# A place of its own for each of 4935 operations in a fused top-k attention and SoLU kernel

## Chip, cores and metric

The kernel runs on one core of one Trainium2 chip. The metric is the device time of one execution in microseconds. The core's engines, each with a queue of its own, are TensorE (PE, with its weight loads shown as PEld), ScalarE (ACT), VectorE (DVE), GpSimd (POOL) and SyncE (SP), which issues the DMAs.

## What is computed

Attention over 8 batches and 8 heads with 576 positions of 64 features, where each query keeps only its 32 largest scores; then a block of two matrix products (512 to 1024 to 512) for 4608 tokens, with SoLU and a layer norm between. Shortened:

```python
scores = (1 / 8) * q @ k.T                       # per batch and head, 576 x 576
kth = np.partition(scores, -32, axis=-1)[..., -32:-31]
attn = softmax(np.where(scores >= kth, scores, -1e9))
x = (attn @ v)                                   # heads side by side: 4608 x 512
h = x @ w_in                                     # 512 x 1024
solu = h * softmax(h)
ln = (solu - mean(solu)) / np.sqrt(var(solu) + 1e-6) * g_ln
out = ln @ w_out                                 # 1024 x 512
```

The weights arrive as 64-bit floats and are turned into 32-bit floats on the chip.

## The kernel before

**Steps.** `steps_of` cuts the attention into 32 steps, four per batch. A step takes four blocks of 128 queries (two heads each) and one block of tails, nine score tiles of 128x576 in all, numbered j. `work_of` lists the operations of all steps, with the engine of each, its length, what it must come after, and the buffers it uses. Within a step they are, by line of the kernel:

- `prep_q`, `prep_k`, `prep_t`: PE transposes the inputs into one of two PSUM buffers `tp` (tails into `o`); ACT copies them out and squares them.
- `estimate` (L1938, ten pairs of small matmuls), `length` (L1945, DVE), `root` (L1952, POOL), `begin` (L1957, DVE): a first guess of each row's threshold.
- `scores` (L1984, PE into two PSUM buffers `big`), `evac` (L1993, ACT copies to `X`), `exps` (L2115, ACT).
- `count0` (L2001 on DVE, L2009 on ACT): how many scores lie above the guess; `second`, `moved`, `even` (L2027, L2036, L2043, DVE): the guess corrected; `twice` (L2051).
- `count1` (L2058, nine on ACT): signs and count at the new guess; `side` (L2067, DVE, tile `al`, three for three counts each), `nearest` (L2079) and `best` (L2090): the scores next to it; `merged`, `which`, `chosen`, `kth`: the 32nd score.
- `keep` (L2160, DVE): the exponentials above the threshold, with their sum; `inverse`; `turn_r`, `copy_r`, `rd_out`, `rd_in`: the inverse sums go through DRAM to be spread over partitions.
- `transpose_p` and `transpose_last` (L2237, L2268 to L2272, PE into `tp`), `copy_p` and `copy_last` (L2250, L2253, L2276, ACT to `PT`), `attn_v` (L2293), `attn_t` (L2302, PE), `copy_v` (L2316, L2323, DVE to `xTm`, `xTt`).

**Tokens.** For each of 36 blocks of 128 tokens: `mm1` (L2334), `hexp` (L2345), `solu` (L2353), `square` (L2363), `spread` and `ln` (POOL), `transpose_ln` (L2384), `copy_ln` (L2390), `mm2` (L2395), `store` (L2402), `send`. They follow the steps of their batch and overlap the attention of the next.

**Weights.** 16 pieces: `load_w`, `w_bits` and `w_corr` (DVE, L1723 to L1739), `w_sum` (L1746, PE into `tp`), `w_copy` (ACT, L1753). At the end they are loaded again and checked (`w_again`, `w_exp`, `w_check`), and `w_verdict` (L2426) decides whether the general path behind the fast one is run; it isn't with these inputs.

**What sets the order.** `arranged(work, rank)` plays the list through while the kernel is built: each engine takes, among the operations that could start soonest, the one with the lowest rank. `PATIENCE` says how much later than the soonest an operation may start and still be taken, and `TURNING` is added to the rank of a PE operation that uses the array in another way than the last one (mode `f` the whole array, `r` two row halves, `c` two column halves). The result is one list; the kernel makes its instructions in that list's order. For PE, ACT, DVE and POOL it is kept as written, as a fixed order in each engine's queue. The rank of an operation is a base (36000 times its step) and a place from the table `PLACES`. The table has rows of its own for the first 8 pairs of heads, 5 tokens and 4 steps and for the last steps and tokens; all others share one row per kind (the keys one per position among four pairs), so that the steps in the middle repeat one pattern.

Of the kernel before, what the change touches and what calls it, by code (L numbers as in the profile page):

```python
# [470 lines left out]
SINGLE = ()  # L471
# [22 lines left out]
def work_of(B, NP, steps, NF, w_wide):  # L494
# [7 lines left out]
    add = w.add  # L502
# [7 lines left out]
    for b in range(B):  # L510
        for hp in range(NP):
            n = pair(b, hp)
# [12 lines left out]
    for i, (b, chunks) in enumerate(steps):  # L525
# [7 lines left out]
        add(("estimate", i), "PE", 450,  # L533
# [94 lines left out]
    tokens = []  # L628
# [32 lines left out]
    for n in range(NW):  # L661
        if w_wide:
# [5 lines left out]
            add(("w_sum", n), "PE", 1290, [("w_corr", n)], [solu, ("tp", ("w", n))], mode="f")  # L668
# [19 lines left out]
STEP = 36000  # L688


def base_of(steps, tokens):
    firsts = {}
    for i, (b, chunks) in enumerate(steps):
        for c in range(4):
            firsts.setdefault(NPAIR * b + chunks[c][0], i)

    def base(key):
        kind, n = key[0], key[1] if len(key) > 1 else 0
        if kind in KEY_KINDS:
            return firsts[n] * STEP  # L700
        if kind in TOKEN_KINDS:
            b, t = tokens[n][:2]
            if b in SINGLE and t < NPAIR:
                return (NPAIR * b + 1 + t) * STEP
            return (NPAIR * b + 2 + min(t, NPAIR - 1)) * STEP
        if kind in LATE_KINDS:
            return len(steps) * STEP
        if kind in WEIGHT_KINDS:
            return 0
        return n * STEP  # L710

    return base


def class_of(key, tokens):
    kind, n = key[0], key[1] if len(key) > 1 else 0
    if kind in KEY_KINDS:
        return f"K{n}" if n < OWN_KEYS else f"k{n % NPAIR}"
    if kind in TOKEN_KINDS:
        b, t = tokens[n][:2]  # L720
        return f"T{n}" if n < OWN_TOKENS else f"Z{t}" if b == 7 and LAST_OWN else "tt" if t == NPAIR else "t"
    if kind in LATE_KINDS or kind in WEIGHT_KINDS:
        return "w"
    return f"S{n}" if n < OWN_STEPS else f"Z{n}" if n >= 30 and LAST_OWN else "s"


def rank_of(steps, tokens):
    base = base_of(steps, tokens)

    def rank(key):  # L730
        c = class_of(key, tokens)
        n = key[1:] if c == "w" else key[2:]
        return base(key) + PLACES[key[0]][c][n[0] if n else 0]

    return rank


NPAIR = 4
OWN_KEYS = 8
OWN_TOKENS = 5  # L740
OWN_STEPS = 4
LAST_OWN = True
KEY_KINDS = ("load_k", "load_t", "tail_square", "load_v", "prep_t", "prep_tc", "prep_k", "prep_kc", "key_square", "key_stats")
TOKEN_KINDS = ("mm1", "hexp", "solu", "square", "spread", "ln", "transpose_ln", "copy_ln", "mm2", "store", "send")
WEIGHT_KINDS = ("load_g", "turn_g", "copy_g", "load_w", "w_bits", "w_corr", "w_sum", "w_copy", "w_gain")
LATE_KINDS = ("w_again", "w_exp", "w_check", "w_passed", "w_verdict")


def arranged(work, rank):
# [23 lines left out]
    while len(start) < len(ops):  # L773
# [55 lines left out]
    "load_k": {  # L829
        "K0": [-1716811],  # L830
        "K1": [-245828],
        "K2": [227792],
        "K3": [-1429884],
        "K4": [-8176],
        "K5": [-3062009],
        "K6": [-1412841],
        "K7": [-355373],
        "k0": [-1030779],
        "k1": [-1442591],
        "k2": [-382990],  # L840
        "k3": [-303896],
    },
    "load_t": {
        "K0": [-1925714],
        "K1": [102180],
        "K2": [351217],
        "K3": [-2648411],
        "K4": [-204768],
        "K5": [-790824],
        "K6": [-509905],  # L850
        "K7": [-633496],
        "k0": [-1338629],
        "k1": [185959],
        "k2": [439884],
        "k3": [-364413],
    },
    "load_v": {
        "K0": [540359],
        "K1": [-296512],
        "K2": [361785],  # L860
        "K3": [-4133787],
        "K4": [119830],
        "K5": [-3768809],
        "K6": [-444902],
        "K7": [-1875983],
        "k0": [-70963],
        "k1": [-1466686],
        "k2": [422237],
        "k3": [-978377],
    },  # L870
    "prep_t": {
        "K0": [-1084188],
        "K1": [-1474755],
        "K2": [436197],
        "K3": [-2991661],
        "K4": [261520],
        "K5": [-8410692],
        "K6": [-269545],
        "K7": [-1284952],
        "k0": [-91862],  # L880
        "k1": [-4832167],
        "k2": [116192],
        "k3": [-1082843],
    },
    "prep_tc": {
        "K0": [-175869],
        "K1": [-749576],
        "K2": [695963],
        "K3": [-590749],
        "K4": [156084],  # L890
        "K5": [-5714526],
        "K6": [515895],
        "K7": [481801],
        "k0": [-18883],
        "k1": [-2857382],
        "k2": [531774],
        "k3": [412231],
    },
    "prep_k": {
        "K0": [22470],  # L900
        "K1": [517997],
        "K2": [206630],
        "K3": [855959],
        "K4": [311821],
        "K5": [515333],
        "K6": [-897320],
        "K7": [558498],
        "k0": [354441],
        "k1": [550664],
        "k2": [55262],  # L910
        "k3": [749511],
    },
    "prep_kc": {
        "K0": [-705698],
        "K1": [-763489],
        "K2": [532998],
        "K3": [-575397],
        "K4": [-76495],
        "K5": [-4692927],
        "K6": [-1267314],  # L920
        "K7": [631286],
        "k0": [-517929],
        "k1": [-1529512],
        "k2": [-275145],
        "k3": [350554],
    },
    "key_square": {
        "K0": [191609],
        "K1": [429176],
        "K2": [760863],  # L930
        "K3": [113498],
        "K4": [256344],
        "K5": [-1494524],
        "K6": [201870],
        "K7": [101078],
        "k0": [253669],
        "k1": [293599],
        "k2": [343170],
        "k3": [792546],
    },  # L940
    "tail_square": {
        "K0": [76491],
        "K1": [-735608],
        "K2": [1119556],
        "K3": [-1902133],
        "K4": [381088],
        "K5": [-6092744],
        "K6": [874126],
        "K7": [-334823],
        "k0": [441766],  # L950
        "k1": [-3610787],
        "k2": [1220737],
        "k3": [-277945],
    },
    "key_stats": {
        "K0": [-37826],
        "K1": [39185],
        "K2": [713784],
        "K3": [-703728],
        "K4": [352435],  # L960
        "K5": [-1754043],
        "K6": [1022931],
        "K7": [84658],
        "k0": [197438],
        "k1": [-1051412],
        "k2": [786942],
        "k3": [-12787],
    },
    "load_q": {
        "S0": [-156811],  # L970
        "S1": [88026],
        "S2": [-178771],
        "S3": [-241569],
        "s": [-131498],
        "Z30": [217192],
        "Z31": [-163285],
    },
    "prep_q": {
        "S0": [-153430],
        "S1": [74761],  # L980
        "S2": [-544548],
        "S3": [-262135],
        "s": [-36141],
        "Z30": [114],
        "Z31": [-408351],
    },
    "prep_qc": {
        "S0": [-97802],
        "S1": [37948],
        "S2": [51332],  # L990
        "S3": [-101542],
        "s": [-100332],
        "Z30": [-417100],
        "Z31": [29777],
    },
    "query_square": {
        "S0": [1057034],
        "S1": [1050943],
        "S2": [1006679],
        "S3": [814969],  # L1000
        "s": [1193871],
        "Z30": [830474],
        "Z31": [906169],
    },
    "estimate": {
        "S0": [-352846],
        "S1": [61002],
        "S2": [-381815],
        "S3": [37651],
        "s": [-110145],  # L1010
        "Z30": [-174418],
        "Z31": [-370193],
    },
    "length": {
        "S0": [104761],
        "S1": [481856],
        "S2": [313281],
        "S3": [306525],
        "s": [70425],
        "Z30": [-20069],  # L1020
        "Z31": [131569],
    },
    "root": {
        "S0": [-449277],
        "S1": [-186121],
        "S2": [-235754],
        "S3": [-268864],
        "s": [-296482],
        "Z30": [-476424],
        "Z31": [-165276],  # L1030
    },
    "begin": {
        "S0": [-966568],
        "S1": [-845257],
        "S2": [-1066062],
        "S3": [-482811],
        "s": [-533664],
        "Z30": [-1047582],
        "Z31": [-1088684],
    },  # L1040
    "scores": {
        "S0": [-121302, -924421, -715935, -656232, -1101903],
        "S1": [-474433, -984979, -614471, -429193, -118328],
        "S2": [-992219, -774707, -474374, -231896, -220838],
# [1466 lines left out]
```

## Time and profile before

| | us |
|---|---|
| median of 3 runs | 1246.11 (1245.06 to 1247.51) |
| profiled execution | 1244.19 |
| span of its records | 1242.4 |

| engine | busy in the middle, 186 to 1178 us (992 us) | busy in the first 31 us | in the last 33 us |
|---|---|---|---|
| PE | 960.2 | 18.2 | 26.0 |
| DVE | 892.2 | 13.8 | 2.6 |
| ACT | 843.7 | 21.8 | 9.3 |
| POOL | 121.2 | 3.3 | 3.9 |

A profile is one execution. A row of it names a line, an engine, an operation, the written and read tiles, and a count; then its busy time, the mean duration of one, and how long the engine stood idle just before such an instruction, with what ended that idle time. The DMAs moved 64.57 MB, a mean of 52 GB/s, with the DMA engines busy for at most seven tenths of any of the page's 40 slices.

### The profile page before, as it was taken

The page shows a single profiled execution, that of the slowest core. Times are in us where ns is not written, and L with a number is a line of the kernel's source. Part 1 is how long each engine was busy: PE and PEld are TensorE (multiplying, and loading weights), DVE is VectorE, ACT ScalarE, POOL GpSimd, SP SyncE. Part 2 cuts the span into 40 slices and gives each one's busy share as a digit, 9 for nine tenths or more (in the row PEclk, how much of TensorE's full clock was granted, in tenths as well). Part 3 has the DMA queues.
Part 4 walks back from the last instruction along what each step waited for, and adds up shares of the span by engine and source line. Part 5 has one row for each costly group of instructions (what it writes and reads, how often), then busy time and mean ns, then how long its engine had stood idle before and what let it go on. Part 6 is the DMA issues. An engine that isn't in the chain of part 4 may idle for free.

```text
span 1242.4 us, 19028 instructions
## 1 busy us (share of the span) xinstructions
PE 1158.2 (93%) x5868; PEld 656.7 (53%) x5868; DVE 1059.5 (85%) x3113; ACT 1014.7 (82%) x2180; POOL 144.6 (12%) x167
## 2 busy tenths in 40 slices
PE   5586899999999999989999999989999999999997
PEld 3354454555555555555555555555555555554553
DVE  4889999989888988999879888999888888999920
ACT  7799868788887797999877898899877899888642
POOL 1100020201011020210112010110112001120110
PEclk9789999999999999999999999999999999999999
DMA  7321202011120112120120111211120011111510
GB/s 188 90 75 43 88 20 63 11 31 48 47 55 20 38 50 63 33 52 23 35 77 19 39 30 48 64 39 40 30 72 19 31 28 39 56 59 64 171 53 29
DMA packets 111434, 64.57 MB, mean 52 GB/s; under 512 B 90445, under 2 KB 98906, under 8 KB 111322
## 3 DMA queue, kind: packets, MB, share of 16 engines
q1 hardware_dynamic: 111322, 63.25, 18.4%
q8 instruction: 49, 0.80, 0.3%
q14 instruction: 63, 0.52, 0.2%
HBM read 53.65 MB, written 9.57 MB: 51 GB/s over the span
## 4 chain that ended last, share of the span: by engine, by line
PE 59%; ACT 22%; DVE 15%; issue 2%; DMA 0%; POOL 0%; ACTq 0%; DVEq 0%; SPq 0%
PE o_ps L2395 15%; PE h_ps L2334 14%; PE s_ps L1984 9%; PE om L2293 8%; PE tp_p L2237 6%; ACT sg L2058 4%; ACT X L1993 4%; DVE E L2160 3%; DVE w L2090 3%; ACT E L2115 3%; ACT PT L2250 3%; DVE w L2079 3%; DVE junkv L2001 2%; PE om L2302 2%; ACT junka L2009 2%
## 5 line engine op out<-in xcount | busy, mean ns | idle before, releaser
L2395 PE MATMUL o_ps<-w_out,lnT 128*128 128x512 f32 x576 | 257.5, 593 | 0.4 <-DVE xTt L2323 0.2
L2334 PE MATMUL h_ps<-w_in,xTm 128*128 128x512 f32 x512 | 229.3, 593 | 1.6 <-ACT X L1993 1.6
L2090 DVE MAX8 w<-w 128x8 f32<-128x288 f32 x576 | 225.9, 447 | 0.4
L2058 ACT ACTIVATE sg<-X,t 128x576 bf16<-128x576 f32 x256 | 196.9, 775 | 18.3 <-DVE t L2043 18.3
L2079 DVE SCALAR_TENSOR_TENSOR w<-X,al,sg 128x576 f32<-128x576 f32 x256 | 204.8, 824 | 2.1 <-ACT junka L1771 1.1
L1993 ACT ACTIVATE X<-s_ps 128x576 f32<-128x576 f32 x256 | 162.2, 660 | 50.4 <-PE s_ps L1984 48.9
L2160 DVE SCALAR_TENSOR_TENSOR E<-X,kth,E 128x576 f32<-128x576 f32 x256 | 200.5, 814 | 1.8 <-ACT E L2115 0.6
L2001 DVE TENSOR_SCALAR_CACHE_REDUCE junkv<-X,t 128x576 bf16<-128x576 f32 x216 | 174.6, 808 | 16.4 <-ACT X L1993 8.0
L1984 PE MATMUL s_ps<-kT,qT 64*128 64x288 f32 x1024 | 167.3, 435 | 3.7 <-ACT X L1993 3.7
L2237 PE MATMUL tp_p<-ident,E 128*128 128x128 f32 x1024 | 154.3, 280 | 17.7 <-ACT PT L2250 5.7
L2395 PEld LDWEIGHTS o_ps<-w_out,lnT 128*128 128x128 f32 x576 | 105.0, 190 | 111.9 <-issue 109.9
L2250 ACT COPY PT<-tp_p 128x512 f32<-128x512 f32 x256 | 148.2, 596 | 9.7 <-PE tp_p L2237 9.3
L2237 PEld LDWEIGHTS tp_p<-ident,E 128*128 128x128 f32 x1024 | 116.2, 142 | 74.0 <-issue 30.8
L2115 ACT ACTIVATE E<-X 128x1152 f32<-128x1152 f32 x128 | 149.6, 1179 | 0.4 <-PE tp_p L2237 0.2
L2334 PEld LDWEIGHTS h_ps<-w_in,xTm 128*128 128x128 f32 x512 | 93.0, 190 | 99.3 <-issue 96.3
L2293 PE MATMUL om<-PT,vm 128*64 128x256 f32 (+1 forms) x1024 | 139.0, 417 | 6.6 <-DVE t L1957 3.0
L1984 PEld LDWEIGHTS s_ps<-kT,qT 64*128 64x128 f32 x1024 | 94.1, 189 | 59.6 <-issue 26.1
L1952 POOL TENSOR_TENSOR zs<-zs,phalf 128x9 f32<-128x9 f32 x32 | 60.3, 1885 | 459.4 <-DVE zs L1945 459.4
L2293 PEld LDWEIGHTS om<-PT,vm 128*64 128x64 f32 x1024 | 69.6, 138 | 63.4 <-issue 12.7
L2369 POOL TENSOR_SCALAR var<-var 128x1 f32<-128x1 f32 x36 | 11.4, 318 | 608.0 <-ACT e_sb L2363 595.0
L2363 ACT ACTIVATE e_sb<-solu,nmu 128x1024 f32<-128x1024 f32 x36 | 41.3, 1149 | 27.3 <-DVE nmu L2357 23.8
L2067 DVE SCALAR_TENSOR_TENSOR al<-n,tt 128x3 f32<-128x3 f32 x96 | 15.0, 157 | 55.9 <-ACT sg L2058 55.8
(144 smaller groups left out, 1526.2 us busy)
## 6 DMA issues: line engine op xcount, KB each, us to landing
km<-in_k_dram SPq DMA_DIRECT2D x32, 256.0 KB
q_sb<-in_q_dram SPq DMA_DIRECT2D x128, 64.0 KB
vm<-in_v_dram SPq DMA_DIRECT2D x32, 256.0 KB
out_dram<-osb SPq DMA_DIRECT2D x32, 256.0 KB
scales<-rows SPq DMA_DIRECT2D x58, 128.0 KB
w_raw<-in_moe_w_in_dram SPq DMA_DIRECT2D x8, 512.0 KB
w_raw<-in_moe_w_out_dram SPq DMA_DIRECT2D x8, 512.0 KB
w_again<-in_moe_w_in_dram SPq DMA_DIRECT2D x8, 512.0 KB
```

The source lines that it names most:

```text
L1984: nc.tensor.matmul(out=big[h][:, half, 0:SH], lhsT=queries_of(i, t)[hd, :], rhs=kT[hd, k0 : k0 + SH], start=True, stop=True,)
L1993: nc.scalar.activation(out=x_of(i, j).rearrange("p (a s) -> p a s", a=2), in_=d.pop(("s", j))[:, :, 0:SH], func=AF.Copy, scale=scale,)
L2001: nc.vector.tensor_scalar(out=junk, in0=x_of(i, j), scalar1=st[i][t][:, j : j + 1], scalar2=None, op0=ALU.is_ge, op1=ALU.add, accum_out=co ...
L2058: nc.scalar.activation(out=d["sg", j], in_=x_of(i, j), func=AF.Sign, scale=-(1.0 + 2.0**-23), bias=d["t1"][:, j : j + 1], accum_out=column ...
L2079: nc.vector.scalar_tensor_tensor(out=w, in0=x_of(i, j), scalar=d["al"][:, j : j + 1], in1=d.pop(("sg", j)), op0=ALU.subtract, op1=ALU.mult,)
L2090: nc.vector.max(w8[:, j, 8 * half : 8 * half + 8], w[:, half * SH : (half + 1) * SH])
L2115: nc.scalar.activation(out=d["E", t], in_=d["X", t], func=AF.Exp)
L2160: nc.vector.scalar_tensor_tensor(out=e, in0=x_of(i, j), scalar=d["kth"][:, j : j + 1], in1=e, op0=ALU.is_ge, op1=ALU.mult, accum_out=den_a ...
L2237: nc.tensor.transpose(tp[:, c, :], e[:, c * P : (c + 1) * P], ident)
L2293: nc.tensor.matmul(out=o[h * D : (h + 1) * D, cols], lhsT=vm[:, h, c, :], rhs=pt[:, h * NM + c, :], start=(c == 0), stop=False,)
L2334: nc.tensor.matmul(out=h[:, half, :], lhsT=x[:, c, :], rhs=w_in[:, c, half * 512 : (half + 1) * 512], start=(c == 0), stop=(c == NP - 1),)
L2395: nc.tensor.matmul(out=o, lhsT=d["lnT"][:, c, :], rhs=w_out[:, c, :], start=(c == 0), stop=(c == NF - 1),)
```

## The change

`rank_of` with its bases and shared rows is taken out. `PLACES` now holds one number for each operation, found by the operation's own key, and that number alone is its rank. `PATIENCE` and `TURNING` become 0, so that among the operations that could start soonest the lowest place wins. Two lengths in the planner's list are set anew. `arranged`, the makers of the instructions, the buffers and the dependences stay.

```diff
-        add(("estimate", i), "PE", 450,
+        add(("estimate", i), "PE", 300,
...
-            add(("w_sum", n), "PE", 1290, [("w_corr", n)], [solu, ("tp", ("w", n))], mode="f")
+            add(("w_sum", n), "PE", 1560, [("w_corr", n)], [solu, ("tp", ("w", n))], mode="f")
...
-    def rank(key):
-        c = class_of(key, tokens)
-        n = key[1:] if c == "w" else key[2:]
-        return base(key) + PLACES[key[0]][c][n[0] if n else 0]
...
+def place_of(key):
+    places = PLACES[key[0]]
+    for n in key[1:]:
+        places = places[n]
+    return places
...
 PLACES = {
...
-    "side": {
-        "S0": [-1225990, -1004058, -1472440],
-        "S1": [-907195, -897390, -974162],
-        "S2": [-988574, -699495, -808215],
...
+    "side": [
+        [50837, 816, -28229],
+        [-18683, 69915, 58524],
+        [197812, 57921, 126612],
...
-PATIENCE = {"PE": 171, "ACT": 56, "DVE": 0, "POOL": 18243, "SP": 1014}
-TURNING = 352098
+PATIENCE = {"PE": 0, "ACT": 0, "DVE": 0, "POOL": 0, "SP": 0}
+TURNING = 0
...
-        for kind, *args in arranged(work, rank_of(steps, order_of_tokens)):
+        for kind, *args in arranged(work, place_of):
```

The lists that result differ all along, by small moves. The first loads that SP issues, as an example: before km, the tails (q, then k), w_raw, km, q_sb; after it w_raw, the tails, km, q_sb, w_raw. On PE the first operations before are prep_t.0, prep_k.0, scores.0, prep_k.1, prep_q.0, w_sum.0, two of scores.0, prep_t.1, estimate.0; after it prep_t.0, prep_k.0, w_sum.0, prep_q.0, two of scores.0, prep_k.1, scores.0, prep_t.1, w_sum.1, estimate.0.

## The prediction

> **What bounds the kernel now.** Forecast: about 15 us less, 1231 us. The page's busy times, slices and chain come first.
>
> ```profile
> span 1242.4 us, 19028 instructions
> ...
> PE 1158.2 (93%) x5868; PEld 656.7 (53%) x5868; DVE 1059.5 (85%) x3113; ACT 1014.7 (82%) x2180; POOL 144.6 (12%) x167
> ...
> PE   5586899999999999989999999989999999999997
> ...
> DVE  4889999989888988999879888999888888999920
> ...
> PEclk9789999999999999999999999999999999999999
> ...
> PE 59%; ACT 22%; DVE 15%; issue 2%; DMA 0%; POOL 0%; ACTq 0%; DVEq 0%; SPq 0%
> ```
>
> Three engines share the load: PE holds most of the chain but ACT and DVE 37% of it, so it changes engine again and again. Next the table by stages, for the steady part alone:
>
> ```profile
> 186.00:1178.00 992.00, 960.20 (x4907) 546.60 (x4907) 892.15 (x2628) 843.74 (x1807) 121.21 (x119) 1.00 0.17 46
> ```
>
> PE is busy 960.2 of 992 us and idle 31.8. Here a rule speaks **against** the change: an engine 97% busy has nothing to win from order. The Trainium skill (Perfetto Trace Analysis, Identifying the Most-Contended Engine) says that matmul busy time is no measure of PE's headroom, because matmuls are pipelined. The timeline of the tail agrees:
>
> ```profile
> 1190.77 13.90 PE L2334 MATMUL h_ps<-w_in,xTm 128*128 128x512 f32 x32
> ```
>
> 32 of these take 13.90 us, so one starts every (13.90 - 0.59)/31 = 429 ns, though the page gives 593 ns as its duration. By such start intervals (429 ns at 512 columns, 243 at 288, 109 at 128, 25 for an estimate, half for the paired heads) all of PE's work is 1047 us, and 885 us in the steady part. So 107 us of it is not work: 50 us stand at the 270 changes between the array's three uses (whole array, row pairs, column pairs), some 150 ns each in the median, which leaves 56 us of waits. By the busy row order can win at most 32 us there, by the intervals 107; I use the second.
>
> The waits, from the groups by line (busy, mean ns, then idle before and who ended it):
>
> ```profile
> L1993 ACT ACTIVATE X<-s_ps 128x576 f32<-128x576 f32 x256 | 162.2, 660 | 50.4 <-PE s_ps L1984 48.9 <-ACT lnT L2390 0.5 <-ACT Et L2115 0.3
> ...
> L2237 PE MATMUL tp_p<-ident,E 128*128 128x128 f32 x1024 | 154.3, 280 | 17.7 <-ACT PT L2250 5.7 <-ACT PT L2276 5.1 <-ACT PT L2253 1.6
> ...
> L2067 DVE SCALAR_TENSOR_TENSOR al<-n,tt 128x3 f32<-128x3 f32 x96 | 15.0, 157 | 55.9 <-ACT sg L2058 55.8
> ```
>
> and from the list of who waited for whom (total, times, longest):
>
> ```profile
> PEld tp_p L2237 <- ACT PT L2250: 18.3, 35, 1.1
> ...
> DVE t L1957 <- POOL zs L1952: 7.6, 8, 2.0
> ```
>
> DVE's one large wait is al (`side`) for the sign counts on ACT, 55.8 us. PE's are short waits for one of the two `tp` buffers, until ACT has copied it out. All idle of PE at `tp` groups that ACT ended (tp_p, tp_ln, tp_pt, tp_r, tp_qk, w_tp) adds up to 28.3 us.
>
> **The change, part by part.** Every instruction stays, so no term comes from durations; what moves is what stands between an instruction and the one it waits for. I counted that in the two orders of operations, each operation with the length that the planner's table gives it, which the trace confirms where it matters (a count 765 ns there, 196.9 us / 256 = 769 in the trace; four transposes 436, and 4 x 109).
>
> 1. *al behind the counts (DVE).* After `even` (L2043), ACT needs three counts of 0.77 us, 2.3 us, and what stands between them, before the first al can run; DVE must have other work queued for as long. In the old order 17 of 32 steps have 0.6 us or less between the two, in the new one 7. Per step I took cover less ACT's queue from the first count to the third count that an al needs, and kept the largest shortfall: the sum is 61.6 us before (the trace shows 55.8, so the count is fair) and 43.9 after. Scaled: 55.8 x (1 - 43.9/61.6) = **-16.0 us on DVE**. Behind al stand nearest, best and the rest of the step.
> 2. *begin behind root (DVE).* L1957 waits for POOL's 1.89 us power, itself released by L1945. With 2.0 us needed, the shortfall grows from 10.5 to 13.4 us (trace: 7.6 before): **+2.9 us on DVE**. Behind it stand the first counts.
> 3. *The two tp buffers (PE).* Fill n+2 needs the copy of fill n: 0.16 us for the last matmul's end, 0.60 for the copy, some 0.1 for signals, so about 0.9 us of other PE work must lie between. The old order has less in 93 of 539 places, short by 31.5 us in all (28.3 seen); the new one in 41, by 14.6. Scaled: 28.3 x (1 - 14.6/31.5) = **-15.2 us on PE**.
> 4. *Array changes (PE).* 327 before, 317 after; 10 x 0.15 = **-1.5 us on PE**. The old planner held 352098 against a change of use; the new one holds nothing, yet the places bring fewer.
> 5. *Evictions and exps (ACT).* Counts stand 0.7 us earlier in ACT's queue on average, evictions (L1993) 0.7 us earlier too, copies 0.3 later, exps (L2115) 2.4 later. An exps is first needed by keep, which stands behind kth; DVE's idle before keep is 1.8 us in 256. Cost 0; if that cover were gone, at most 2.4 us in some steps.
> 6. *The head.* SP's queue now begins with the 512 KB w_raw, ahead of the tails, km and q. In the trace w_raw was issued at 3.58 us and used at 8.30, so it can be ready near 5.4. km falls from first to fourth: its issue goes from 0.72 to about 3.3 us, and with the 4.7 to 5.3 us from issue to use that the first two km show, prep_k moves from 5.4 to about 8.3. But the first estimate, which starts the counts, ran at 19.0 after w_sum.0 and three scores paced by ACT; in the new queue w_sum.0 and w_sum.1 fill the early time, and estimate.0 again comes near 19. I take 0, between -1.5 (one w_sum less later) and +3 (the km delay in full). The rule that weighs here is the clock gate's (the Trainium skill, TensorE: Matmul & The Clock Gate, Part 1): after an idle window of about 3.4 us PE runs at half clock for as long again, about 1.7 us lost. The trace agrees: after 11.0 us of idle at 27-38 us two matmuls of w_tp took 2.07 us, against 1.12 warm. Four waits over 3.4 us stand in the first 100 us; one more or less is 1.7 us either way, inside my ends.
> 7. *The tail.* After the last copy_v (1191 us) three tokens stay in both orders, with PE full. The verdict's matmul moves from before the last mm2 to after it; the loads of `bad` then run beside the last store's landing (issued 1235.7, seen at 1240.5), so 0; without that cover about 1 us.
> 8. *The planner's numbers* (estimate 300, w_sum 1560, patience 0) issue nothing: 0.
>
> PE sums to -16.7, DVE to -13.1. They don't add: both pass the same 32 steps, and what one saves beyond the other becomes a new wait for it. The common gain lies between 0 (all taken up elsewhere) and 29.8 (places wholly apart). The chain alternates, so some places are apart, which makes up for savings that are swallowed; I take the middle of the two engines, 15. The profiled execution took 1244.2 us (span 1242.4): 1244.2 - 15 = 1229.2. The runs shown have a median 1.9 us higher: **1231**. Late next will be ACT: X waiting for scores, and what is left of al.
>
> **The rivals.**
> - *Both gains count in full*, since the places lie apart: 1246.1 - 29.8 = 1216. For it: the chain's many turns. Against it: a step needs both engines. Chance 0.17; my forecast, 1224 to 1238, 0.57.
> - *The gain goes off the path*: scores come no earlier, ACT stays idle before X, and only the array changes count: 1244.6. For it: 48.9 us of X waiting for PE. Against it: PE's own shortfalls halve. Chance 0.14, spread from 1238 to 1248.
> - *Slower, by PSUM slots of scores.* A count served early can hold an eviction behind it by 0.66 us, and PE's next scores with it (two `big` buffers). One eviction per step on the path is 32 x 0.66 = +21.1; if DVE's saving is then worth nothing and PE keeps -16.7 only by half, 1246.1 + 21.1 - 8.4 = 1259. It decides from 0.26 us a step (8.4/32). For it: the X row above. Against it: evictions stand earlier on average. Chance 0.12, mostly in milder forms, 1249 to 1259.
>
> **How the numbers follow.** A measurement here tells about 0.2%, 2.5 us. Faster by more than that: 0.57 + 0.17 + 0.08 of the third = 0.82; same 0.06; slower 0.12. The range leaves out the farther part of the full-gain case and most of the slower one: 1217 to 1246.
>
> **What would show it.** Right: al's idle before it near 40 us, PE's idle at ACT-ended tp groups near 13, array changes 317, DVE's last copy_v near 1176 instead of 1191, busy times unchanged, w_raw used near 5.4 us. Wrong: PE's idle before s_ps for X well above 4 us, X waiting much longer than 49, DVE's end not earlier, or a head that reaches its first count later than 25 us.

## The result, and the profile after

The changed kernel takes **1203.62 us** in the median of 4 runs (1203.29 to 1204.33), against 1246.81 (1245.06 to 1248.30) in 4 runs of the kernel before: a ratio of 0.9655, 95% interval 0.9638 to 0.9672, or 43.2 us less. The direction was forecast, the size was not: 15 us were expected, and the time lies below the 1217 to 1246 us given.

The page of the kernel after (busy time and share of the span, then the slices, then the chain by engine):

```profile
span 1201.9 us, 18981 instructions
...
PE 1147.5 (95%) x5866; PEld 661.0 (55%) x5868; DVE 1047.0 (87%) x3113; ACT 1011.2 (84%) x2180; POOL 149.9 (12%) x167
...
PE   6676999999999999999999999999999999999997
...
PEclk9689899999999999999999999999999999999999
...
PE 58%; DVE 23%; ACT 14%; issue 2%; POOL 1%; DMA 1%; SPq 0%; DVEq 0%; ACTq 0%
```

Busy times are as before within some 13 us, and the work is the same, so what the span lost, 40.5 us, was waiting, shown as idle or inside the busy time. The chain is as mixed as before: ACT's part fell from 22% to 14%, DVE's rose from 15% to 23%, and PE kept its share. No engine has become the one bound.

The same stretch of the steady part as before, moved forward by the 40.5 us at its end (stretch, its length, then busy time and instructions of PE, PEld, DVE, ACT, POOL):

```profile
186.00:1137.50 951.50, 943.33 (x4908) 545.74 (x4908) 880.08 (x2622) 839.42 (x1798) 126.21 (x119) 1.00 0.17 48
```

Nearly the same instructions (4908 on PE against 4907, 2622 on DVE against 2628) now take 951.5 us instead of 992. PE's idle time fell from 31.8 to 8.2 us, DVE's from 99.9 to 71.4, ACT's from 148.3 to 112.1. PE's visible idle fell by 23.6 us, its busy time by 16.9, with the same work: of what a stretch of PE loses, a good part is written down as busy.

The groups by line (busy and mean duration, then idle time before and what ended it):

```profile
L2223 ACT ACTIVATE X<-s_ps 128x576 f32<-128x576 f32 x256 | 159.1, 664 | 41.9 <-PE s_ps L2214 41.1 <-ACT PT L2480 0.3
...
L2467 PE MATMUL tp_p<-ident,E 128*128 128x128 f32 x1024 | 151.3, 279 | 17.8 <-ACT PT L2480 6.2 <-ACT PT L2506 3.3 <-ACT w_in L1983 2.9
...
L2297 DVE SCALAR_TENSOR_TENSOR al<-n,tt 128x3 f32<-128x3 f32 x96 | 14.3, 155 | 29.0 <-ACT sg L2288 28.6
```

and who waited for whom (total, times, longest):

```profile
DVE t L2187 <- POOL zs L2182: 11.9, 15, 2.0
...
PE s_ps L2214 <- ACT X L2223: 0.8, 1, 0.8
```

The last of these was, in the kernel before:

```profile
PE s_ps L1984 <- ACT X L1993: 6.9, 15, 1.6
```

DVE's wait at al (L2067 before, L2297 now: the new lines are 230 higher) halved, 55.8 to 28.6 us. ACT waits 7.8 us less for scores, and PE's own wait for a scores buffer, 6.9 us before, is all but gone. PE's visible idle at tp_p, where I expected most of PE's gain, did not move over the whole span: 17.7 to 17.8. But this is a sum of two stages. In the same row, taken from 186 us on, it fell from 11.5 to 5.4, and in the first 186 us it rose from 6.2 to 12.4.

To see where PE's time went I took, from both traces, the time from each matmul's start to the next and subtracted the matmul's own interval, as in the prediction. From the first matmul to the last it is 1229.6 us before and 1189.6 after, of which work is 1047 in both. What is left:

| time between PE starts that is not work, us | before | after |
|---|---|---|
| changes of array use (95 or 200 ns allowed each) | 50.5 | 49.3 |
| at `tp` groups, first 186 us | 43.0 | 36.7 |
| at `tp` groups, later | 44.5 | 22.6 |
| at scores | 20.9 | 17.7 |
| at attention times v (`om`) | 11.3 | 5.5 |
| at mm1, mm2, estimates, tails | 12.5 | 10.8 |
| all | 182.7 | 142.7 |

The `tp` groups lost 87.5 us before and 59.3 after. They gave back 28.2 of the 40 us, 21.9 of these after the head. This tells where PE waits, not yet for whom: a group of transposes can wait for its buffer or for the `keep` of DVE whose result it turns.

### The profile page after: what moved, and what is told of

The parts are those of the page before. It is cut to its first block, busy times and chain, and to the rows that moved or that the text cites. A ratio compares the mean times of both kernels' runs of the same rounds, so it can differ in the third digit from the quotient of the medians.

```text
span 1201.9 us, 18981 instructions
## 1 busy us (share of the span) xinstructions
PE 1147.5 (95%) x5866; PEld 661.0 (55%) x5868; DVE 1047.0 (87%) x3113; ACT 1011.2 (84%) x2180; POOL 149.9 (12%) x167
## 3 DMA queue, kind: packets, MB, share of 16 engines
q1 hardware_dynamic: 111322, 63.25, 18.8%
## 4 chain that ended last, share of the span: by engine, by line
PE 58%; DVE 23%; ACT 14%; issue 2%; POOL 1%; DMA 1%; SPq 0%; DVEq 0%; ACTq 0%
PE o_ps L2625 16%; PE h_ps L2564 11%; PE s_ps L2214 10%; PE tp_p L2467 7%; PE om L2523 7%; DVE junkv L2231 5%; ACT sg L2288 4%; DVE w L2320 4%; DVE w L2309 4%; DVE E L2390 4%; ACT E L2345 2%; PE tp_ln L2614 2%; PE tp_qk L2087 2%; PE om L2532 2%; ACT PT L2480 2%
## 5 line engine op out<-in xcount | busy, mean ns | idle before, releaser
L2320 DVE MAX8 w<-w 128x8 f32<-128x288 f32 x576 | 224.1, 446 | 0.3
L2288 ACT ACTIVATE sg<-X,t 128x576 bf16<-128x576 f32 x256 | 196.5, 778 | 12.6 <-DVE t L2273 12.1
L2309 DVE SCALAR_TENSOR_TENSOR w<-X,al,sg 128x576 f32<-128x576 f32 x256 | 202.0, 815 | 0.9
L2223 ACT ACTIVATE X<-s_ps 128x576 f32<-128x576 f32 x256 | 159.1, 664 | 41.9 <-PE s_ps L2214 41.1
L2214 PE MATMUL s_ps<-kT,qT 64*128 64x288 f32 x1024 | 170.1, 440 | 1.6 <-ACT X L2223 0.8
L2467 PE MATMUL tp_p<-ident,E 128*128 128x128 f32 x1024 | 151.3, 279 | 17.8 <-ACT PT L2480 6.2
L2625 PEld LDWEIGHTS o_ps<-w_out,lnT 128*128 128x128 f32 x576 | 105.1, 190 | 111.1 <-issue 110.3
L2182 POOL TENSOR_TENSOR zs<-zs,phalf 128x9 f32<-128x9 f32 x32 | 63.2, 1976 | 507.2 <-DVE zs L2175 500.0
L2214 PEld LDWEIGHTS s_ps<-kT,qT 64*128 64x128 f32 x1024 | 96.7, 191 | 52.8 <-issue 24.2
L2599 POOL TENSOR_SCALAR var<-var 128x1 f32<-128x1 f32 x36 | 12.7, 354 | 514.3 <-ACT e_sb L2593 514.2
L2593 ACT ACTIVATE e_sb<-solu,nmu 128x1024 f32<-128x1024 f32 x36 | 41.5, 1152 | 14.8 <-DVE nmu L2587 14.6
L2575 ACT ACTIVATE e_sb<-h_ps 128x1024 f32<-128x1024 f32 x36 | 36.7, 1020 | 19.9 <-PE h_ps L2564 19.8
```

The lines of the kernel that those rows point to most:

```text
L2214: nc.tensor.matmul(out=big[h][:, half, 0:SH], lhsT=queries_of(i, t)[hd, :], rhs=kT[hd, k0 : k0 + SH], start=True, stop=True,)
L2288: nc.scalar.activation(out=d["sg", j], in_=x_of(i, j), func=AF.Sign, scale=-(1.0 + 2.0**-23), bias=d["t1"][:, j : j + 1], accum_out=column ...
L2309: nc.vector.scalar_tensor_tensor(out=w, in0=x_of(i, j), scalar=d["al"][:, j : j + 1], in1=d.pop(("sg", j)), op0=ALU.subtract, op1=ALU.mult,)
L2320: nc.vector.max(w8[:, j, 8 * half : 8 * half + 8], w[:, half * SH : (half + 1) * SH])
L2467: nc.tensor.transpose(tp[:, c, :], e[:, c * P : (c + 1) * P], ident)
L2625: nc.tensor.matmul(out=o, lhsT=d["lnT"][:, c, :], rhs=w_out[:, c, :], start=(c == 0), stop=(c == NF - 1),)
```

## The experiments

Each kernel computes the same result. Where the order is set by hand, the new kernel's file takes its operations from a fixed list in place of the planner:

```diff
-        for kind, *args in arranged(work, place_of):
+        named = list(work.ops)
+        for kind, *args in [named[n] for n in ORDER]:
```

Only ORDER differs between such kernels. "Counted" is the prediction's way of adding up what stands between an operation and the one it waits for. The time after is 1203.6 throughout. Ratios are to the runs of the kernel before that were taken along; their medians lie between 1246.8 and 1248.4, so a difference to 1203.6 is good to some 1.5 us.

**Where: the head or all steps?** `head_new` takes the new list up to the last keep of step 6 and the old order for the rest; `head_old` the reverse.

> The new list up to the last keep of step 6 (the first 290 us or so), then the rest in the old order. Theory A, the gain is spread over all steps (the new profile is some 12 us ahead at this point, of 43 at the end): 1233 to 1237 us. Theory B, the head starts the gain and the old pattern carries it on: 1205 to 1215. Theory C, what the head gains is lost again in the steady part, which has its own bound: 1244 to 1248.

> The old list up to the last keep of step 6, then the rest in the new order. Theory A (spread over all steps): 43 - 12 = 31 us gained, 1214 to 1218 us. Theory B (the head starts it): 1235 to 1245. Theory C (the steady part has its own bound): 1203 to 1206.

Measured: 1239.16 (0.9928, 0.9911 to 0.9946) and 1216.91 (0.9752, 0.9703 to 0.9801), which is 9.3 and 31.5 us below the 1248.43 of the kernel before beside them. `head_new` ends 2 us past the range of theory A, `head_old` inside it. Together they give 40.8 of the 43 us. The gain is not one of the head: 9.3 us in the first seven of 32 steps and 31.5 in the other 25, in both parts 1.3 us a step on average.

**Which engine: each queue's order alone.** `new_pe_act` keeps the new order in PE's and ACT's queues and the old in DVE's, `new_dve` the reverse; ORDER takes the ready operation that is lowest in its own queue's chosen list.

> PE's and ACT's queues in the new order, DVE's in the old one as far as dependences let it. Counted in this list: cover missing before al 93.7 us (before 61.6, after 43.9), tp shortfall 23.8 us (31.5, 13.9). Theory 1, PE's and ACT's order brings the gain and DVE only follows: 1210 to 1220 us. Theory 2, DVE's order brings it: 1240 to 1250. Theory 3, an order is worth something only together with the other queues' orders: 1255 or more, slower than before.

> DVE's queue in the new order as far as dependences let it, PE's and ACT's in the old one. Cover missing before al 115.3 us, tp shortfall 39.6 us. Theory 1 (PE's and ACT's order): 1240 to 1250 us. Theory 2 (DVE's order): 1215 to 1225. Theory 3 (only together): 1260 or more.

Measured: 1501.91 (1.2038, 1.1978 to 1.2098) and 1527.83 (1.2247, 1.2186 to 1.2308), far worse than both kernels. From the waits of `new_dve`:

```profile
DVE al L2297 <- ACT sg L2288: 170.6, 49, 11.9
...
ACT PT L2480 <- PE tp_p L2467: 111.1, 59, 7.7
```

The al wait is three times that of the kernel before, and ACT's wait for transposes, 9.3 us before, is 111.1. The counts for these lists (al 93.7 and 115.3, tp 23.8 and 39.6) explain a part of the 250 to 280 us at most: theory 3 has the sign, and nothing foresaw the size. Within each kernel the queues' orders are fitted to each other; a mix tells nothing of what either half is worth.

**The planner's rules or the places?** `rules_zero` is the kernel before with the new PATIENCE and TURNING, `rules_old` the new kernel with the old ones.

```diff
-PATIENCE = {"PE": 171, "ACT": 56, "DVE": 0, "POOL": 18243, "SP": 1014}
-TURNING = 352098
+PATIENCE = {"PE": 0, "ACT": 0, "DVE": 0, "POOL": 0, "SP": 0}
+TURNING = 0
```

> The old shared places, with patience and turning cost 0 as in the new kernel. Counted: al 42.7 us missing (as good as new), tp shortfall 44.6 us (worse than the old 31.5), 346 changes of the array (327). Theory R, the gain comes from the simpler rules: 1205 to 1225 us. Theory D (al is time): about 1232. Theory P (tp and changes are time): 13 + 3 us more, 1262.

> The new places, with the old patience and turning cost. Counted: al 84.3 us missing, tp shortfall 59.7 us, 314 changes. If the places carry the gain whatever the rules: 1204 to 1215 us. If places and rules belong together: slower than the old kernel, 1260 or more.

Measured: 1426.29 (1.1418, 1.1382 to 1.1454) and 1499.68 (1.2028, 1.2004 to 1.2052). The idea that the old places held back by the rules were the loss falls with the first: without the rules they are 180 us worse. No theory had that. The counts for this list, al as good as new and tp 13 us worse than old, allowed 1262 at most. So the counts price small changes of one fitted list, as in the runs that follow; they do not tell how good another list is. In `rules_old` DVE starves for evicted scores, a wait of 7.0 us in the kernel after:

```profile
DVE junkv L2231 <- ACT X L2223: 171.1, 76, 12.3
```

Places and rules are one setting in each kernel.

**One wait at a time.** These keep the new list and move few operations. In `al_back` 100 DVE operations that stood between even and the first al go behind that al (counted: 43.9 up to 90.5 us); `al_half` moves 33 of them, to come back to the old count, 61. In `tp_back` 26 PE operations, 25 of them `scores`, that stood between two fills of `tp` go behind the second or a later one, in 31 moves (counted: 13.9 up to 28.3). The prediction's 14.6 is the same count as this 13.9, but with `estimate` at 300 ns, where its 31.5 has 450; all counts of tp here have 450. In ORDER, by the example of one step:

```diff
-even, <other DVE work>, twice, the first al, ...
+even, twice, the first al, <other DVE work>, ...
```

> The new order with 100 moves on DVE alone: work that stood between even and the first al goes behind al. The cover missing before al rises from 43.9 to 90.5 us. Theory D, DVE sets the pace and waits on al are time: +30 us or more, 1234 or later. The prediction's first step with its halving: +15 to +20, 1219 to 1223. Theory P, PE sets the pace and DVE has room: under +6, 1204 to 1210.

> The new order with 31 moves on PE alone: a piece of work that stood between two fills of the tp buffers goes behind the second. The counted shortfall at the tp buffers rises from 13.9 to 28.3 us (before: 31.5). Theory P, the prediction's third step (a shortfall at tp is time): +13 us, 1216. Theory J, PE is late or early by other queues and a single buffer wait is mostly taken up by the next: under +5 us, 1204 to 1208.

> The new order with DVE's moves undone in part only: the cover missing before al is 61.2 us, the old kernel's 61.6 (new 43.9), tp as in the new. By what 100 moves cost (49.5 us for 46.6 counted): 17.3 x 1.06 = +18, about 1222 us. If the first microseconds are covered by PE's work (the prediction's halving): +9 or less, 1212.

Measured: `al_back` 1253.15 (1.0049, 1.0034 to 1.0064), `tp_back` 1222.78 (0.9803, 0.9784 to 0.9822), `al_half` 1223.05 (0.9807, 0.9791 to 0.9824). A counted microsecond at al costs (1253.15 - 1203.62)/46.6 = 1.06 in the first and 19.4/17.3 = 1.1 in the third. One at tp costs 19.2/14.4 = 1.33, more than either theory had. Nothing of either is swallowed. From the waits of `al_back`:

```profile
DVE al L2297 <- ACT sg L2288: 93.8, 33, 4.6
```

65.2 us more than after, for 49.5 us of time: a part of the visible wait is free, but nearly all of the counted one is not. In `al_half` the same wait is

```profile
DVE al L2297 <- ACT sg L2288: 57.0, 23, 4.1
```

From the waits of `tp_back`:

```profile
ACT X L2223 <- PE s_ps L2214: 49.3, 60, 2.7
DVE al L2297 <- ACT sg L2288: 35.7, 24, 4.1
```

No operation of ACT or DVE has been moved here, yet ACT waits 8.2 us more for scores and DVE 7.1 more at al. PE's delay runs through the other two engines. Since the operations put back are nearly all `scores`, the 1.33 is the price of late scores together with that of the buffer wait; this run does not part them.

**Do they add?** `both_half` makes the moves of `al_half` and of `tp_back` (al counted 61.2, tp 28.3).

> The moves of al_half and those of tp_back together: al 61.2 and tp 28.3 us short, both near the old kernel's. Theory add (waits on DVE and on PE lie apart, each is time): al_half's rise plus 19, near 1241 us. Theory middle (the prediction: what one saves beyond the other becomes a wait for it): the larger of the two alone, near 1223 us.

Measured: 1241.57 (0.9948, 0.9928 to 0.9968), 38.0 us above the kernel after; the two alone gave 19.4 + 19.2 = 38.6. From its waits:

```profile
DVE al L2297 <- ACT sg L2288: 65.8, 26, 4.2
ACT X L2223 <- PE s_ps L2214: 55.2, 57, 5.0
```

Both waits stand there together, each larger than where it was brought back alone (57.0 us at al in `al_half`, 49.3 at X in `tp_back`). **They add in full.** 33 moved operations on DVE and 26 on PE, of 4935, return 38 of the 43 us, with the 317 changes of array use left as they are.

The traces show how. ACT's list is the same in all four kernels, so its instructions can be set against those of the kernel after one by one. The lag of each rises in jumps and stays flat in between. At the instruction that starts at 733 us in the kernel after, `al_half` is 11.0 us late, `tp_back` 12.7 and `both_half` 24.2; at 1081 us it is 18.6, 18.0 and 37.6. From 200 us on, the lag (the median of 60 instructions in a row) never shrinks by more than 0.2 us. What is lost at one wait is not made up at a later one, neither there nor on another engine, and so the two sum.

PE's loss at the `tp` groups, by start intervals as in the table above, rises by 16.7 us in `tp_back`, by 11.6 in `al_half`, where PE's list is untouched, and by 29.2 in both. That is about the 28.2 us that these groups gave back: some two fifths of it are DVE's lateness, which PE meets there.

**Does each engine set the pace?** Three kernels add about the same work to one engine, spread over the steps, with the new order untouched; two do it to the kernel before. Each addition was put on a chain that other engines wait for.

```diff
 # PE: two of the eight groups of transposes done twice, 27.9 us
+            if j in (1, 5):
+                nc.tensor.transpose(tp[:, c, :], ...)
 # DVE: one tile's two maxima done twice, 25.0 us
-            nc.vector.max(...)
+            for _ in range(2 if j == 4 else 1):
+                nc.vector.max(...)
 # ACT: every second step two copies, else one, done twice, 27.8 us
-        nc.scalar.copy(...)
+        for _ in range(2 if j == 1 or j == 5 and i % 2 else 1):
+            nc.scalar.copy(...)
```

> The new kernel with two groups of four transposes done twice in each step, which gives the same result: 8 x 109 ns x 32 = 27.9 us more PE work. If PE sets the pace alone: +28, 1231 us. If the engines hand the pace round and each microsecond on any of them is time: +28 as well, but then DVE's addition costs as much. If DVE sets it: under +10.

> The new kernel with the two MAX8 of one tile done twice in each step, which gives the same result: 0.78 x 32 = 25 us more DVE work, on DVE's way from the counts to kth. If PE sets the pace alone: under +8, 1204 to 1212 us. If the engines hand the pace round (theory add): +20 to +25, 1224 to 1229 us.

> The new kernel with one copy of transposed probabilities done twice in each step, a second one in every other step, same result: 48 x 0.58 = 27.8 us more ACT work, on the way that frees a tp buffer. If all three engines hand the pace round: +18 to +28, 1222 to 1232 us. If ACT has room (84% busy): under +10, 1213.

> The same 27.9 us of PE work as in after_more_pe, in the old kernel. In the new one it cost 19.9. If in the old order, too, PE's work is nearly all time: +18 to +24, 1265 to 1271 us. If the old order's larger waits cover it (the ground for the prediction's halving): under +12, 1259.

> The same 25 us of DVE work as in after_more_dve, in the old kernel. In the new one it cost 25.0. If DVE's work is time in the old order too: +20 to +25, 1267 to 1272 us. If the old order's waits cover it: under +12, 1259.

| work added | us added | kernel after: us, ratio (95%) | longer by | kernel before: us, ratio (95%) | longer by |
|---|---|---|---|---|---|
| PE | 27.9 | 1223.51, 0.9815 (0.9797 to 0.9833) | 19.9 | 1262.70, 1.0117 (1.0086 to 1.0147) | 14.8 |
| DVE | 25.0 planned, 31.7 found | 1228.67, 0.9852 (0.9834 to 0.9870) | 25.0 | 1271.29, 1.0194 (1.0165 to 1.0223) | 23.4 |
| ACT | 27.8 | 1221.62, 0.9788 (0.9763 to 0.9813) | 18.0 | not run | |

PE's and ACT's additions have the planned size in the traces (PE's 256 transposes start 109 ns apart, ACT's copies are busy for 27.4 us more). DVE's is larger. The maxima in the kernel after and with the addition:

```profile
L2320 DVE MAX8 w<-w 128x8 f32<-128x288 f32 x576 | 224.1, 446 | 0.3
...
L2321 DVE MAX8 w<-w 128x8 f32<-128x288 f32 x640 | 253.6, 448 | 2.5
```

That is 29.5 us of busy time and 2.2 of idle, 31.7 us in all; in the kernel before it is 31.6. So the 25.0 us that the kernel got longer are not the whole of what was added, though they equal the plan.

All three engines are on the path at once, in the kernel after and, as far as it was run, in the one before. In the kernel after DVE, busy for 87% of the span, passes on about four fifths of what it is given, PE at 95% seven tenths, ACT at 84% two thirds; in the kernel before DVE three quarters and PE half. PE's two runs lie between their theories.

**The kernel before with its tp count mended.** `old_tp_fix` takes the old order and brings 12 PE operations forward (three `scores`, six token products, two `prep_t`, one `estimate`), to stand between two fills. The count falls from 31.5 to 26.2.

> The old order with 12 moves on PE alone, each putting a piece of work between two fills of the tp buffers: shortfall 26.2 us instead of 31.5, changes of the array 325 instead of 327. By tp_back's rate (19.2 us for 14.4 counted) 5.3 x 1.33 = -7, 1240 us. If a wait taken away by hand in the old order is made up elsewhere: 1245 to 1248.

Measured: 1268.55 (1.0154, 1.0128 to 1.0179), 20.7 us slower, a plain miss. From its waits:

```profile
PEld s_ps L2214 <- ACT X L2223: 25.0, 43, 2.4
...
PE s_ps L2214 <- ACT X L2223: 11.8, 20, 2.2
```

The first of these was, in the kernel before (the second is shown above, 6.9):

```profile
PEld s_ps L1984 <- ACT X L1993: 17.0, 34, 2.1
```

By start intervals PE loses 20.7 us at scores after the head (9.0 before) and 13.5 at token products (3.6), while the `tp` groups lose 89.0 (87.5). DVE's list is the same in both kernels, so the lag can be followed here too. It comes in jumps at the moved operations and is flat between them (12.5 to 12.6 us from 418 to 533 us); of 25.3 us between the two profiled executions, 8.6 come at two of the moved `scores` and some 14 at five of the token products. The scores found their own buffer not yet evicted: those of step 15 hold PE for 3.7 us, 1.5 before. A token product takes 3.4 us, and the group of transposes that it overtakes comes 3.0 to 3.6 us later than it would have, to cover a wait of under 0.9. A count of one wait's cover says nothing of the wait of the operation that is to be the cover, nor of those that it overtakes.

## Why the prediction was wrong in size

**Right.** What bounds the kernel: three engines on one chain, with the losses of PE read by start intervals and not by its busy row. The mechanism, too: al falls, and so does PE's loss at `tp`. Array changes went to 317, DVE lost 4.3 us more at begin (7.6 to 11.9; +2.9 was forecast). The head was costed at 0; from the trace of the kernel after (start, duration, engine, what; in brackets the idle before):

```profile
4.42 0.43 DVE L1953 TENSOR_SCALAR w_tmp<-w_raw 128x512 uint32<-128x512 uint32 x1 [2.49 <-DMA w_raw<-in_moe_w_in_dram]
...
6.61 1.12 PE L2087 MATMUL tp_qk<-ident,km 128*128 128x128 f32 x4 [1.10 <-DMA km<-in_k_dram]
...
7.52 1.92 PE L1976 MATMUL w_tp<-w_tmp,ident 128*128 128x512 f32 x2
```

w_raw is used at 4.42 us (5.4 was forecast) and km at 6.61 (8.3 forecast, 5.42 before). The first begin stands at 20.5 us against 21.6, inside the ends given for it. The tail cost nothing, as forecast: the verdict's last sum on DVE (n_ok) waits 19.2 us for its matmul, and nothing waits for it.

**The step that failed** is the sum: "They don't add: both pass the same 32 steps, and what one saves beyond the other becomes a new wait for it", and with it "I take the middle of the two engines, 15". `both_half` shows the reverse: 38.0 together for 38.6 one by one. `al_half` alone, at 19.4, is more than the 15 given to both. Of the 28 us that the forecast was short, 15 are this step (29.8 - 15). The rival "both gains count in full", held at 0.17, was right in its mechanism; at 1216 it was still 13 us short, because of the sizes of its terms:

| term | predicted | estimate from the rates of `al_back`, `al_half`, `tp_back` |
|---|---|---|
| al, counted 17.7 us less (61.6 to 43.9) | 16.0 | 17.7 x 1.06 to 1.1 = 18.8 to 19.5 |
| tp, counted 17.6 us less (31.5 to 13.9; the prediction's 16.9 mixes two lengths of `estimate`) | 15.2 | 17.6 x 1.33 = 23.4 |
| both | 15 taken, 31.2 if added | 42.2 to 42.9, of 43.2 in all |

The tp term is the one most mis-sized. By scaling to "28.3 seen" I priced a counted microsecond at 28.3/31.5 = 0.9; `tp_back` shows 1.33. I also read the idle row over the whole span. With its smaller parts the idle of the tp groups that ACT ended is 30.3 us before, and it is 23.9 after, where I had expected near 13. By stages it fell from 17.4 to 6.1 behind 186 us, about as forecast, and as the start intervals have it there (44.5 to 22.6), and rose from 12.9 to 17.9 in front of it. Two smaller slips: 50 us at 270 changes of array use are 185 ns each, not 150, so the term of changes should have been -1.9; and the clock's term does not come out.

The prediction quotes a rule for the clock and counts waits over 3.4 us, at an estimated 1.7 us each. In the first 100 us there are four before and three after, so the clock should have been no worse. But it stood at half in five stretches against four in the first 103 us, and for 41.0 us against 34.1 up to 241 us, as far as the two traces record it. In the kernel after half clock set in at 51.6, 99.4 and 119.9 us, next to idle stretches of 2.0, 2.9 and 2.6 us at most: a wait of 3.4 us is not needed for it.

The signs I had named: al near 40, found 28.6; the last copy_v near 1176, found in the timeline of the kernel after at

```profile
1150.76 0.41 DVE L2546 TENSOR_TENSOR xTm<-om,scales 128x256 f32<-128x256 f32 x1
```

that is 40.3 us earlier than the 1191.07 of the kernel before, so the whole gain was made before the tail. "Late next will be ACT" was half the story: ACT's wait for scores fell as well (48.9 to 41.1), since scores came sooner on a PE that waited less.

The rival of the slower side, PSUM slots of scores, is refuted for this change: PE's wait there fell from 6.9 to 0.8 us. But it is a real mechanism: the two `scores` that met it stand for 8.6 of the 25.3 us by which the profiled `old_tp_fix` is slower.

**Left open.** How the 1.33 for a microsecond counted at tp divides between the buffer and the late scores, and where in full the 250 us of the mixed orders stand, is not settled. The planner's two new lengths were not tried alone. Whether the gain needs a place for each operation, or a better list with shared places would do, can't be told from these runs.

## What to carry over

When a loop passes through several engines that each show waits, ask first whether a saving on one is passed on whole: add a known amount of work to each engine in turn. Where two or three of them hand most of it to the time, expect savings at separate waits to add, as they did here, and take neither the larger nor a middle without a reason. Check in the trace how large the added work came out. Follow the lag of the same instructions between two traces: if it never shrinks, nothing is made up, and each jump names the move that made it. Read idle rows and start intervals stage by stage, since a sum over the whole span hid the fall here. Before moving an operation to cover a wait, count the wait of that operation itself and the length by which it puts off those that it overtakes.

## What was not expected of the hardware

- DVE, idle for 13% of the span, passed 25.0 of 31.7 added us to the time, and ACT, idle for 16%, 18.0 of 27.8. At these places an idle share of that size was hardly any slack.
- The maxima done twice cost more than the first time: some 1.0 us for the two repeats on a tile (31.7/32), where two maxima are otherwise busy for 0.78 us (2 x 224.1/576).
- The longest idle stretch of PE in the head, 11.0 us before w_tp at 27 to 38 us, is gone in the kernel after, yet the clock granted between 31 and 93 us is 0.78 there against 0.82. PE's idle time in this stretch is nearly the same, 16.8 us against 17.5, in shorter waits (the longest 4.2 at tp_p). PE's loss at `tp` in the first 186 us fell by only 6.3 us.
- The mean granted clock fell from 0.98 to 0.91 in the two mixed orders (0.907 and 0.906), where PE waits longer and oftener. That the waits lower the clock is inferred; no run here changes them alone.
